# One list of token slots made apart from the others, maxima of k by pairwise operations, and a new hand order of a kernel's prologue

## The chip, the cores and the metric

The kernel runs on one core of a Trainium2 chip. A core has five engines, each with its own queue of instructions that it works off in order: TensorE (PE; matmuls and transpositions, with its weight loads shown as PEld), VectorE (DVE), ScalarE (ACT), GpSimd (POOL) and SyncE (SP, which here only issues DMAs). Engines wait for each other through semaphores. The metric is the device time of one execution in microseconds (us), and the number given for a kernel is a median over runs. The profile and the trace come from one profiled execution.

## The reference, cut to what matters

Three stages follow each other: a linear attention over 4 batches with 8 heads of 64 and 576 tokens, a mixture of 8 experts of which each of the 2304 tokens takes two, and a feed-forward stage with a rational function.

```python
q_s = softmax(q over head_dim)                     # q, k, v: (4, 8, 576, 64)
k_s = np.exp(k - np.max(k, axis=2, keepdims=True)) # the maximum over the 576 tokens
k_s = k_s / (k_s.sum(axis=2, keepdims=True) + 1e-9)
kv  = einsum('bhsd,bhse->bhde', k_s, v)
x   = einsum('bhsd,bhde->bhse', q_s, kv)           # -> (2304, 512)

noisy = x @ w_gate + log1p(exp(x @ w_noise)) * noise
top2  = the two largest of the 8 noisy logits of a token; weights: softmax over the two
for e in range(8): for k in range(2):
    mask = top2[:, k] == e
    out[mask] += weight[mask, k] * (relu(x[mask] @ w1[e]) @ w2[e])     # w1 512x1024, w2 1024x512

h = out @ w_in;  g = P(h) / (Q(|h|) + 1e-6);  return g @ w_out         # P cubic, Q quadratic
```

## The kernel before

**Stages.** The prologue (to about 127 us of the span) does the attention, the gate, the routing and expert 0's first 256 tokens. Then come expert 0's later tokens, experts 1 to 7 in blocks of up to 384 tokens, and the last stage. From the first block on, TensorE's queue is little else than matmuls, three for each product (lines 757 to 759: the operands are split into a high and a low part).

**The order.** In the prologue the order on every engine is written by hand: the string `ORDER` names steps (`name.index`), and each step appends its instructions to the queues of the engines that it uses. `LOADS` does the same for the first DMAs on SP's queue, and `REST` for what is left behind expert 0's `prep`. Behind the prologue a scheduler places instructions, and `issue_after` holds a group back behind a named mark.

**Steps of the attention.** Of a batch b, `km` holds 512 tokens of k as 128 partitions x (8 heads, 4 rows r, 64) and `kr` the 64 tokens left over. `krT`/`krm` find the leftover's maxima, `kmx` (L272) reduces the four rows r on VectorE, `kmT` transposes that on TensorE into a PSUM tile (`keyb`, which cycles through three), `kmm` reduces over partitions (L284, L285), `kmB` spreads the maxima into a PSUM tile `pm`, `ksb` subtracts them (`ek`, `kr`; L298, L301), `kex` takes exponentials on ScalarE (L305), `ksm` sums on POOL, `kv` multiplies with v (`pk`; weights are `vm` and `vr`), `kz`/`kvn` divide, `kvT`/`kvc`/`kg`/`kgc` make from it the matrix `kvx` that yields outputs and gate logits at once (`pg` is its gate part). For q, `qmx` (L369: `mx`), `qsb`, `qex`, `qsm` (`qs`), `qse`, `qrc` and `qnm` are the softmax. For each of 18 token tiles, `xT` transposes q (`qT`, two PSUM tiles), `xc` copies it on ScalarE (`qTs`), `xp` multiplies with `kvx` (`px`, one PSUM tile), `xo` copies the outputs on ScalarE, `xs` stores them to `Xrows` in DRAM and `xg` sums the gate logits `L` on VectorE (L458). `aw`, `sa` and `sv` load and split expert 0's weights (`w10h`, `w10l` and so on, in halves of 128x1024).

**Steps of the routing.** The tokens are taken in two halves, g = 0 and 1, of 9 tiles. `route` (`rt.g`) makes the noisy logits, the two largest, the counts (`rt`, L555, and the matmuls `base`), positions and then, in three groups of 3 tiles, one-hots on VectorE: `route<-route,itC` (L585) and `ocv` (L591) for the list's columns and `oh` (L594, 128x768) for its 128 rows. There are 48 columns: 6 for each of the 8 experts. `fill_list` (`rl.g`) multiplies them on TensorE into one `list` in PSUM (18 matmuls of 96 columns). From g = 0 come the indices `gidxA` of expert 0's first 256 tokens, from g = 1 the indices `gidxE` of its later 384 and, ordered by the experts' sizes (`ranks`), `gidx` for experts 1 to 7. `weights` (`rw.g`) makes the gate's weights.

**Expert 0.** `ag` gathers its first tokens (`xga`), `at`/`ac`/`al` transpose and split them (`xTa`, `xa`), `m1`/`mb` are the first product (`pha`), `mr`/`ml` its relu and split, `m2`/`mc` the second (`acca`). `eg` gathers the later ones (`xgb`), the first instruction of which on TensorE is `xT<-ident,xgb` (L803); VectorE splits these into `xl` (L806). Experts 1 to 7 gather by `gidx` (`xg<-Xrows,gidx`, L787), and their weights `raww` are loaded on SP and split by ScalarE (`w10h`, L678) and VectorE (`w10l`, L679).

Of the kernel before, what the change touches and what calls it, by code (L numbers as in the profile page):

```python
# [38 lines left out]
NCOL = E * CC  # L39
# [19 lines left out]
    kg.1 xc.5 xT.4 kgc.1 rsm.0 xp.7 xc.4 krm.1 qse.0 kv.0.3 qrc.0 xo.7 xg.7 qmx.2 xp.4 xo.4 qnm.0.0 kz.0 rmx.1
    xg.4 rnm.0 rex.1 kvn.0 xp.5 qsb.2 xg.5 kmT.3 kmT.2 qmx.3 kvT.0 rse.1 xT.0 xo.5 xT.8 kvc.0 xp.6 kmm.3 qsb.3  # L60
    xc.0 xg.6 aw.0.0 kmB.3 kmm.2 xo.6 kg.0 xc.8 rsm.1 ksb.3 kmB.2 kgc.0 qex.2 xp.0 qnm.0.3 xs.4 xo.0 xs.6 rnm.1
    xg.0 xT.3 kex.3 ksb.2 xp.8 xs.7 qnm.0.2 xs.0 qnm.0.1 xs.5 xT.2 qex.3 kv.3.0 aw.0.1 ksm.3 xg.8 qsm.2 kv.3.1
    xc.2 xo.8 qsm.3 qse.2 xp.2 xc.3 xs.8 kex.2 aw.1.0 xT.1 kv.3.2 qrc.2 xg.2 qnm.2.2 kz.3 qse.3 xo.2 qnm.2.3
# [1253 lines left out]
```

## Time and profile before

| | us |
|---|---|
| median of 3 runs | 975.9 (974.28 to 1564.1) |
| the profiled execution | 974.89 |
| its span, first to last instruction | 972.9 |
| TensorE busy in the span | 941.4 (97%) |
| VectorE busy | 757.7 (78%) |
| ScalarE busy | 591.0 (61%) |
| POOL busy | 281.7 (29%) |

A row of the timeline has the start, the duration, the engine, the line, the operation and out<-in; in brackets behind it stand the idle time of that engine just before and what ended it. `PEld` rows are TensorE's weight loads, `SPq` rows the issues of DMAs. Names are those of the program without the batch or tile number, so `px` is the projection of some tile.

### The profile page before, as it was taken

The page shows a single profiled execution, that of the slowest core. Times are in us where ns is not written, and L with a number is a line of the kernel's source. Part 1 is how long each engine was busy: PE and PEld are TensorE (multiplying, and loading weights), DVE is VectorE, ACT ScalarE, POOL GpSimd, SP SyncE. Part 2 cuts the span into 40 slices and gives each one's busy share as a digit, 9 for nine tenths or more (in the row PEclk, how much of TensorE's full clock was granted, in tenths as well). Part 3 has the DMA queues.
Part 4 walks back from the last instruction along what each step waited for, and adds up shares of the span by engine and source line. Part 5 has one row for each costly group of instructions (what it writes and reads, how often), then busy time and mean ns, then how long its engine had stood idle before and what let it go on. Part 6 is the DMA issues. An engine that isn't in the chain of part 4 may idle for free. (4 is left out here: it accounts for less than half of the span.)

```text
span 972.9 us, 15490 instructions
## 1 busy us (share of the span) xinstructions
PE 941.4 (97%) x5296; PEld 841.8 (87%) x5296; DVE 757.7 (78%) x1552; ACT 591.0 (61%) x1198; POOL 281.7 (29%) x276
## 2 busy tenths in 40 slices
PE   2999899999999999999999999999999999999998
PEld 1888788888988888888989999899899999998997
DVE  6876769676877878778831389989899898798795
ACT  2586245464645556455631387787787877787775
POOL 4888221221302121122121142222323232232221
PEclk9999999999999999999999999999999999999999
DMA  9982168675866758586676591230020000000001
GB/s 265 298 274 80 63 224 250 190 219 170 242 197 214 249 175 259 167 250 216 208 233 201 175 359 34 76 108 23 1 76 1 17 27 1 33 1 1 33 1 33
DMA packets 91147, 137.35 MB, mean 141 GB/s; under 512 B 15698, under 2 KB 44374, under 8 KB 91064
## 3 DMA queue, kind: packets, MB, share of 16 engines
q1 hardware_dynamic: 76536, 100.27, 33.5%
q0 software_dynamic: 14528, 36.05, 11.9%
q8 instruction: 42, 0.69, 0.3%
q14 instruction: 41, 0.34, 0.1%
HBM read 100.64 MB, written 36.05 MB: 141 GB/s over the span
## 5 line engine op out<-in xcount | busy, mean ns | idle before, releaser
L1172 POOL TENSOR_TENSOR hlr<-vr,hhr 128x384 fp32r<-128x384 f32 x95 | 105.1, 1110 | 287.6 <-ACT hhr L1171 212.1
L757 PE MATMUL phr<-xhr,wih 128*128 128x384 f32 x384 | 129.8, 338 | 0.0
L759 PE MATMUL phr<-xhr,wil 128*128 128x384 f32 x384 | 129.3, 337 | 0.0
L758 PE MATMUL phr<-xlr,wih 128*128 128x384 f32 x384 | 129.0, 336 | 0.0
L822 DVE SCALAR_TENSOR_TENSOR hl<-ph,hh 128x256 fp32r<-128x256 f32 (+4 forms) x120 | 56.4, 470 | 76.8 <-ACT hh L821 75.6
L821 ACT ACTIVATE hh<-ph 128x256 fp32r<-128x256 f32 (+4 forms) x120 | 50.4, 420 | 106.3 <-PE ph L759 106.2
L758 PE MATMUL accr<-wol,hhr 128*128 128x512 f32 x288 | 113.4, 394 | 0.0
L757 PE MATMUL accr<-woh,hhr 128*128 128x512 f32 x288 | 112.7, 391 | 0.0
L759 PE MATMUL accr<-woh,hlr 128*128 128x512 f32 x288 | 109.6, 395 | 0.0
L1160 DVE SCALAR_TENSOR_TENSOR sqr<-sqr,coef,abr 128x384 f32<-128x384 f32 x96 | 64.2, 668 | 35.3 <-ACT sqr L1159 35.3
L787 POOL DMA_INDIRECT xg<-Xrows,gidx x35 | 39.5, 1128 | 158.9 <-PE xT L803 156.5
L1155 ACT ACTIVATE vr<-phr,coef 128x384 f32<-128x384 f32 x96 | 64.1, 668 | 33.1 <-PE phr L759 25.1
L1167 DVE SCALAR_TENSOR_TENSOR sqr<-sqr,qone,abr 128x384 f32<-128x384 f32 x96 | 71.7, 747 | 9.4 <-ACT abr L1166 5.2
L749 POOL DMA_INDIRECT Yrows<-y,sidx x35 | 38.9, 1113 | 136.9 <-ACT y L842 128.6
L1165 ACT ACTIVATE abr<-sqr,qone 128x384 f32<-128x384 f32 x96 | 59.7, 623 | 26.4 <-DVE sqr L1160 26.2
L757 PE MATMUL ph<-xh,w11h 128*128 128x256 f32 (+4 forms) x240 | 75.3, 314 | 0.0
L757 PEld LDWEIGHTS phr<-xhr,wih 128*128 128x128 f32 x384 | 72.2, 188 | 3.3
L758 PEld LDWEIGHTS phr<-xlr,wih 128*128 128x128 f32 x384 | 72.1, 188 | 3.3
L757 PE MATMUL ph<-xh,w10h 128*128 128x256 f32 (+4 forms) x240 | 72.0, 303 | 1.0 <-ACTq L1087 1.0
L758 PE MATMUL ph<-xl,w10h 128*128 128x256 f32 (+4 forms) x240 | 72.6, 303 | 0.0
L759 PE MATMUL ph<-xh,w11l 128*128 128x256 f32 (+4 forms) x240 | 72.6, 302 | 0.0
L758 PE MATMUL ph<-xl,w11h 128*128 128x256 f32 (+4 forms) x240 | 72.4, 301 | 0.0
(293 smaller groups left out, 2621.1 us busy)
## 6 DMA issues: line engine op xcount, KB each, us to landing
raww<-in_moe_w_dram SPq DMA_DIRECT2D x56, 512.0 KB, 4.5
r64i<-in_moe_w_in_dram SPq DMA_DIRECT2D x32, 256.0 KB, 3.4
r64o<-in_moe_w_out_dram SPq DMA_DIRECT2D x32, 256.0 KB, 3.1
ylr<-Yrows SPq DMA_DIRECT2D x32, 256.0 KB, 3.1
qm<-in_q_dram SPq DMA_DIRECT2D x4, 1024.0 KB, 7.8
vm<-in_v_dram SPq DMA_DIRECT2D x4, 1024.0 KB, 8.1
raw<-in_moe_w_dram SPq DMA_DIRECT2D x4, 1024.0 KB, 7.9
Xrows<-xo SPq DMA_DIRECT2D x16, 256.0 KB, 2.3
```

The costliest lines, as they stand in the source:

```text
L749: st = G.indirect_dma_start(out=Y, out_offset=bass.IndirectOffsetOnAxis(ap=idx, axis=0), in_=yt, in_offset=None, bounds_check=2 * NTOK - 1 ...
L757: PE.matmul(o, ah, bh, start=first, stop=False)
L758: PE.matmul(o, ah, bl, start=False, stop=False)
L759: return PE.matmul(o, al, bh, start=False, stop=last).ins
L787: G.indirect_dma_start(out=g[0:self.rows(t)], out_offset=None, in_=X, in_offset=bass.IndirectOffsetOnAxis(ap=self.cols(gidxE, gidx, t), ax ...
L821: a_ = A.activation(hh, ph, AF.Relu)
L822: v_ = V.scalar_tensor_tensor(hl, ph, 0.0, hh.bitcast(F32), op0=ALU.max, op1=ALU.subtract)
L1155: A.activation(v, ph, AF.Identity, scale=coef[:, 3:4], bias=coef[:, 2:3])
L1160: V.scalar_tensor_tensor(sq, sq, coef[:, 5:6], ab, op0=ALU.mult, op1=ALU.add)
L1165: A.activation(r0, sq, AF.Ln, bias=qone)
L1167: V.scalar_tensor_tensor(sq, sq, qone, r0, op0=ALU.add, op1=ALU.mult)
L1172: (V if self.end and f == NF2 - 1 else G).tensor_tensor(gl, v, gh.bitcast(F32), op=ALU.subtract)
```

## The change

1. **Maxima of k.** `kmx` was one reduction over r. Now `kmp`, a copy on ScalarE, puts row 0 into a PSUM tile (`keyb`), and `kmx` takes three maxima on VectorE, two in place in PSUM and the last from PSUM to SBUF. The steps of batch 1 from `kmp` to `kex` are done in two halves of four heads, and the load of its v comes in two (`vm1a`, `vm1b`).
2. **Expert 0's list.** `route` now makes a position `sE` and a value `vE` of expert 0 alone (at most one of a token's two choices is expert 0, so one entry per token in place of two), one-hots `ohE` of 640 and 512 elements and `ocvE` with 6 columns. `fill_first` (`re.g`) is 9 matmuls of 12 columns into `listE`. `gidxA` and `gidxE` come from it.
3. **The other experts' list.** `general` (`rg.g`) makes the one-hots of the 42 columns left from the positions kept in `pos` and `idf`. `rl.g` multiplies as before (18 matmuls, 84 columns). `ranks` (`rk`) stays in the prologue. For g = 1 nearly all of `rg`, `rl` and the indices `gidx` (`by_rank`, `rf`) stand in `REST`, behind expert 0's `prep`. Tiles that now live longer come from a pool `late`.
4. **Order.** `ORDER` is another one throughout. `REST` is also held behind the marks V and A (VectorE's and ScalarE's last split of expert 0's later tokens).

The core of the diff:

```diff
-    kr0 km1a km1b qm1 km0 - qr0 - vm1 - vr0 - qm0 - vm0 - km2 - kr1 - km3 - qm2 - vm2 - vr1 qr1 qm3 vm3
+    kr0 km1a km1b qm1 km0 - qr0 - vm1a - vm1b - vr0 - qm0 - vm0 - km2 - kr1 - km3 - qm2 - vm2 vr1 qr1 qm3 vm3
...
 REST = """
-    ay.0 mc.6 mc.7 ay.1
+    ay.0 mc.6 mc.7 rg.1 ay.1 rl.1 rl.1 rg.1 rl.1 rg.1 rf
 """
...
+    def kmp(b, h=None):
+        hs = heads(h)[0]
+        t = once("kmp", b, h, lambda: keyb(f"kmp{b}").rearrange("p (h d) -> p h d", h=H))
+        A.activation(t[:, hs], km[b][:, hs, 0, :], AF.Copy)
...
-            V.tensor_reduce(t, km[b].rearrange("p h r d -> p h d r"), axis=AX.X, op=ALU.max)
...
+            for r in range(1, R):
+                V.tensor_tensor(x if r < R - 1 else t, x, src[r], op=ALU.max)
...
+        V.scalar_tensor_tensor(ti, sE, AWAY, pb[:, EA:EA + 1].to_broadcast([P, TP]), op0=ALU.add, op1=ALU.add)
...
+        V.tensor_tensor(ocE, over(tj, CC), itC[:, 0:CC].unsqueeze(1).to_broadcast([P, TP, CC]), op=ALU.is_equal)
...
+        for t0, t1 in ((0, TA), (TA, TP)):
+            V.tensor_tensor(oh[:, t0:t1], tr[:, t0:t1].unsqueeze(2).to_broadcast([P, t1 - t0, P]),
+                            itR.unsqueeze(1).to_broadcast([P, t1 - t0, P]), op=ALU.is_equal)
+            yield
...
+    def fill_first(g):
+
+        lists["E", g] = qTb(f"listE{g}")[:, 0:2 * CC]
+        oh, ocv = ehot[g]
+        for t0, t1 in ((0, TA), (TA, TP)):
+            for t in range(t0, t1):
+                PE.matmul(lists["E", g], oh[:, t, :], ocv[:, t].rearrange("p z c -> p (z c)"),
+                          start=(t == 0), stop=(t == TP - 1))
+            yield
+
+    def general(g):
...
+    def by_rank():
+
+        lr = late.tile([P, NR, CC, NR], F32, name="lr")
+        lw = late.tile([P, NR, CC], F32, name="lw")
...
+        slots(late, lw.rearrange("p r c -> p (r c)"), NR * CC, gidx, sidx, "m")
...
-    with tc.issue_after(marks["xT"]):
+    with tc.issue_after(marks["xT"]), tc.issue_after(marks["V"]), tc.issue_after(marks["A"]):
         rest(REST)
```

Lines behind the new functions have other numbers in the changed kernel (757 to 759 are 843 to 845 there, L458 is L490, L806 is L892).

**First place.** VectorE's queue in the middle of the attention, between the two reductions for batches 2 and 3 and the first `ek` behind them; a digit behind a name is the batch or, for `px`, the tile. Before:

```order
L272 TENSOR_REDUCE kmx2_347<-km2_168 128x512
L272 TENSOR_REDUCE kmx3_374<-km3_175 128x512
L385 TENSOR_REDUCE qs0_390<-eq0_325 128x32
...
L458 TENSOR_REDUCE L_110<-px7_418 128x16
L369 TENSOR_REDUCE mx2_437<-qm2_178 128x32
...
L458 TENSOR_REDUCE L_110<-px5_470 128x16
L369 TENSOR_REDUCE mx3_488<-qm3_190 128x32
L284 TENSOR_REDUCE mr1_425<-kmT3_478 128x4
L285 TENSOR_REDUCE m3_515<-mr1_425 128x4
...
L284 TENSOR_REDUCE mr1_425<-kmT2_483 128x4
L285 TENSOR_REDUCE m2_530<-mr1_425 128x4
...
L298 TENSOR_TENSOR ek3_543<-km3_175,pm3_525 128x8x4x64
```

In the changed kernel:

```order
L401 TENSOR_REDUCE mx0_373<-qm0_169 128x32
L295 TENSOR_TENSOR kmp2_387<-kmp2_387,km2_175 128x512 x2
L295 TENSOR_TENSOR kmx2_389<-kmp2_387,km2_175 128x512
...
L401 TENSOR_REDUCE mx2_429<-qm2_185 128x32
L295 TENSOR_TENSOR kmp3_422<-kmp3_422,km3_182 128x512 x2
L295 TENSOR_TENSOR kmx3_451<-kmp3_422,km3_182 128x512
L490 TENSOR_REDUCE L_113<-px7_459 128x16
...
L417 TENSOR_REDUCE qs0_483<-eq0_403 128x32
...
L313 TENSOR_REDUCE mr1_474<-kmT2_493 128x4
L314 TENSOR_REDUCE m2_510<-mr1_474 128x4
...
L401 TENSOR_REDUCE mx3_527<-qm3_196 128x32
L329 TENSOR_TENSOR ek2_550<-km2_175,pm2_522 128x8x4x64
```

The two reductions for batches 2 and 3 became two pairs of maxima, with `mx` of batches 0 and 2 ahead of them. Batch 3's `mx` stood ahead of both `kmm`, and its `ek` was the first; now batch 2 goes first, and batch 3's `mx` stands directly ahead of batch 2's `ek`.

**Second place.** VectorE's queue from the positions of the second half's tokens to the indices `gidxE` of expert 0's later tokens (`hla` is the split of expert 0's hidden values). Before:

```order
L585 TENSOR_TENSOR route_1054<-route_1054,itC 128x288
L591 TENSOR_TENSOR ocv_0_1201<-route_1054,vhl 128x6x48 x2
L594 TENSOR_TENSOR oh_0_1211<-route_1054,itR 128x768
L585 TENSOR_TENSOR route_1054<-route_1054,itC 128x288
L591 TENSOR_TENSOR ocv_6_1234<-route_1054,vhl 128x6x48 x2
L594 TENSOR_TENSOR oh_6_1244<-route_1054,itR 128x768
L585 TENSOR_TENSOR route_1054<-route_1054,itC 128x288
L591 TENSOR_TENSOR ocv_12_1254<-route_1054,vhl 128x6x48 x2
L594 TENSOR_TENSOR oh_12_1260<-route_1054,itR 128x768
...
L601 TENSOR_TENSOR lfg_1283<-list_1227,lvg_982 128x48
L604 SCALAR_TENSOR_TENSOR route_1054<-list_1227,lfg_1283 128x48
...
L148 SCALAR_TENSOR_TENSOR gidxE<-route_1054,lu_1061 128x6
```

In the changed kernel:

```order
L608 SCALAR_TENSOR_TENSOR route_1130<-sE_1140,base_1238 128x9
L610 TENSOR_SCALAR route_1130<-route_1130 128x9
L611 TENSOR_SCALAR route_1130<-route_1130 128x9
L612 COPY pbs_1268<-base_1238 128x16
L613 TENSOR_TENSOR route_1130<-route_1130,itC 128x54
L615 TENSOR_TENSOR ocvE_1273<-route_1130,vE_1141 128x9x6
L616 TENSOR_TENSOR ocvE_1273<-route_1130,vhl 128x9x6
L620 TENSOR_TENSOR ohE_1276<-route_1130,itR 128x640
...
L620 TENSOR_TENSOR ohE_1276<-route_1130,itR 128x512
...
L625 TENSOR_TENSOR lf_1137<-listE_1293,lvE 128x6
L628 SCALAR_TENSOR_TENSOR route_1130<-listE_1293,lf_1137 128x6
...
L150 SCALAR_TENSOR_TENSOR gidxE<-route_1130,lu_1136 128x6
```

Three groups of one-hots of 768 elements became one of small instructions and two one-hots `ohE` of 640 and 512.

**Third place.** VectorE's queue around the index `gidx` of experts 1 to 7. Before, in the prologue and ahead of expert 0's later tokens:

```order
L490 TENSOR_REDUCE cap_94<-rkt 128x7
L615 TENSOR_TENSOR lr<-lvg_1282,perm 128x294
L618 TENSOR_REDUCE lw<-lr 128x42
L147 TENSOR_SCALAR lum<-lw 128x42
L148 SCALAR_TENSOR_TENSOR gidx<-lw,lum 128x42
...
L993 SCALAR_TENSOR_TENSOR hla<-pha_1275,hha 128x256
L993 SCALAR_TENSOR_TENSOR hla<-pha_1308,hha 128x256
...
L1023 TENSOR_SCALAR coef<-coef 128x4
L806 TENSOR_TENSOR xl_2_1392<-xT_2_0_1393,xh_2_1391 128x4x128
```

In the changed kernel, inside expert 0's block of later tokens (`hl` is the split of its hidden values, `w10l` and `w11l` are splits of expert 1's weights):

```order
L892 TENSOR_TENSOR xl_2_1436<-xT_2_1_1444,xh_2_1435 128x4x128
...
L687 TENSOR_TENSOR oh_0_1413<-list_1394,itR 128x768
...
L687 TENSOR_TENSOR oh_6_1473<-list_1394,itR 128x768
...
L687 TENSOR_TENSOR oh_12_1497<-list_1394,itR 128x768
...
L908 SCALAR_TENSOR_TENSOR hl_2_0_1563<-ph_2_0_1549,hh_2_0_1562 128x384
...
L765 TENSOR_TENSOR w10l_1577<-raww_1_1578,w10h_1576 128x1024
...
L765 TENSOR_TENSOR w10l_1577<-raww_1_1618,w10h_1576 128x1024
L694 TENSOR_TENSOR lfg_1505<-list_1480,lv_135 128x42
...
L704 TENSOR_TENSOR lr<-lv_136,perm 128x294
L706 TENSOR_REDUCE lw<-lr 128x42
...
L765 TENSOR_TENSOR w11l_1679<-raww_1_1680,w11h_1678 128x1024
L150 SCALAR_TENSOR_TENSOR gidx<-lw,lum 128x42
```

The index moved from ahead of the first split `xl` to behind three one-hot groups, two splits of hidden values and three splits of weights.

## Rows read from the trace of the kernel before

**Rows 1.** Stretches: us, busy PE, PEld, DVE, ACT, POOL (count); clock, DMA share, GB/s

```profile
42.00:50.00 8.00, 6.15 (x28) 5.84 (x27) 6.65 (x12) 3.93 (x19) 5.29 (x3) 0.66 1.01 272
50.00:84.00 34.00, 32.87 (x247) 30.05 (x247) 26.56 (x82) 27.25 (x43) 30.62 (x23) 0.95 0.62 204
84.00:104.00 20.00, 16.14 (x126) 13.86 (x125) 10.88 (x36) 9.90 (x22) 15.15 (x10) 0.96 0.40 123
104.00:127.00 23.00, 21.67 (x154) 19.17 (x154) 21.33 (x98) 3.65 (x11) 3.79 (x5) 1.00 0.15 47
127.00:973.00 846.00, 840.84 (x4604) 752.62 (x4602) 659.76 (x1303) 529.89 (x1076) 200.19 (x186) 1.00 0.43 133
126.70:148.20 21.50, 21.25 (x113) 19.23 (x112) 14.40 (x36) 11.51 (x20) 4.46 (x5) 1.00 0.73 236
```

**Rows 2.** Timeline, the last projections before expert 0

```profile
97.18 0.48 PEld L431 LDWEIGHTS qT<-ident,eq 128*128 128x128 f32 x4
...
98.41 1.03 PEld L444 LDWEIGHTS px<-kvx,qTs 128*128 128x128 f32 x8 [0.75 <-DVE L L458]
...
99.75 0.60 ACT L363 ACTIVATE xo<-px 128x512 f32<-128x512 f32 x1 [1.08 <-issue]
...
100.65 1.25 PE L444 MATMUL px<-kvx,qTs 128*128 128x144 f32 x8 [0.99 <-DVE L L458]
...
103.72 0.39 PE L757 MATMUL pha<-xa,w10h 128*128 128x256 f32 x1 [0.95 <-ACT xa L968]
```

**Rows 3.** VectorE by line, 0 to 60 us: busy, mean ns | idle

```profile
L272 DVE TENSOR_REDUCE kmx<-km 128x512 f32<-128x2048 f32 x4 | 14.8, 3731 | 1.1 <-DMA km<-in_k_dram 1.1
L298 DVE TENSOR_TENSOR ek<-km,pm 128x2048 f32<-128x2048 f32 x4 | 9.1, 2270 | 0.0
L369 DVE TENSOR_REDUCE mx<-qm 128x32 f32<-128x2048 f32 x4 | 9.1, 2263 | 0.0
...
L301 DVE TENSOR_TENSOR kr<-kr,pm 64x512 f32<-64x512 f32 x3 | 2.1, 684 | 0.1
```

**Rows 4.** Timeline, the last q load and the products with v

```profile
40.83 2.18 SPq L195 DMA_DIRECT2D qm<-in_q_dram  x1
...
57.83 1.91 ACT L305 ACTIVATE ek<-ek 128x2048 f32<-128x2048 f32 x1
...
60.52 0.97 PEld L317 LDWEIGHTS pk<-vm,ek 128*128 128x128 f32 x8
...
62.02 0.97 PEld L317 LDWEIGHTS pk<-vm,ek 128*128 128x128 f32 x8
```

**Rows 5.** DMA issues of the page: count, KB each, us to landing

```profile
raww<-in_moe_w_dram SPq DMA_DIRECT2D x56, 512.0 KB, 4.5
...
qm<-in_q_dram SPq DMA_DIRECT2D x4, 1024.0 KB, 7.8
```

**Rows 6.** Timeline, the list of the second half and behind it

```profile
109.15 0.21 DVE L555 TENSOR_REDUCE rt<-route 128x8 bf16<-128x72 f32 x1
...
113.98 0.95 DVE L594 TENSOR_TENSOR oh<-route,itR 128x768 bf16<-128x768 int32 x1
...
115.46 0.43 PE L630 MATMUL list<-ocv,oh 128*128 128x96 bf16 x6
...
116.20 0.95 DVE L594 TENSOR_TENSOR oh<-route,itR 128x768 bf16<-128x768 int32 x1
...
120.65 0.17 DVE L148 SCALAR_TENSOR_TENSOR gidxE<-route,lu 128x6 int32<-128x6 f32 x1
...
125.33 0.20 DVE L148 SCALAR_TENSOR_TENSOR gidx<-lw,lum 128x42 int32<-128x42 f32 x1
...
126.70 1.04 PE L803 MATMUL xT<-ident,xgb 128*128 128x128 f32 x8
...
135.65 1.23 DVE L679 TENSOR_TENSOR w10l<-raww,w10h 128x1024 fp32r<-128x1024 f32 x1 [0.39 <-ACT w10h L678]
```

**Rows 7.** Gathers by gidx, 118 to 165 us

```profile
DMA to landing us min/median/max: 3.8/6.7/6.9
```

More of the change, by code (lines that the diff above doesn't have):

```diff
@@ L38 @@
 CC = 6
-NCOL = E * CC
+NCOL = (E - 1) * CC
+TA = 5
+AWAY = 8192.0
 G2E = 2 * E
@@ L59 @@
[L59 to L63, printed above, removed]
@@ L267, in over_r, with heads @@
             eng.tensor_tensor(t, t, src[r], op=op)
-    def kmx(b, eng=None):
-        t = st["kmx", b] = pw.tile([P, H, HD], F32, tag="kmx", name=f"kmx{b}", bufs=2)
-        if eng is None:
-            V.tensor_reduce(t, km[b].rearrange("p h r d -> p h d r"), axis=AX.X, op=ALU.max)
-        else:
-            over_r(eng, t, [km[b][:, :, r, :] for r in range(R)], ALU.max)
-    def kmT(b):
-        pt = st["kmT", b] = keyb(f"kmT{b}").rearrange("p (c t) -> p c t", c=NHP)
-        for c in range(NHP):
+    def heads(h):
+        return [slice(None)] * 3 if h is None else [slice(h * n, (h + 1) * n) for n in (H // 2, NHP // 2, 2 * P)]
@@ L279, in kmT, with pairs, kmm @@
+    def pairs(h):
+        return range(NHP)[heads(h)[1]]
+    def kmT(b, h=None):
+        pt = once("kmT", b, h, lambda: keyb(f"kmT{b}").rearrange("p (c t) -> p c t", c=NHP))
+        for c in pairs(h):
             PE.transpose(pt[:, c, :], half(st["kmx", b], c), ident)
-    def kmm(b):
-        m = st["m", b] = pw.tile([P, NHP], F32, tag="m", name=f"m{b}", bufs=2)
+    def kmm(b, h=None):
+        cs = heads(h)[1]
+        m = once("m", b, h, lambda: pw.tile([P, NHP], F32, tag="m", name=f"m{b}", bufs=2))
@@ new lines, in route @@
+        le = lists["E", g]
+        if g:
+            V.tensor_tensor(lf, le[:, CC:], lvE, op=ALU.add)
+        else:
+            V.tensor_copy(lf, le[:, CC:])
+        V.scalar_tensor_tensor(lvp, le[:, 0:CC], 64.0, lf, op0=ALU.mult, op1=ALU.add)
+        if g:
+            slots(None, lvp, CC, gidxE, sidxE, "e", (lt, lu))
+        else:
+            slots(None, lvp[:, 0:NA], NA, gidxA, sidxA, "a", (lt[:, 0:NA], lu[:, 0:NA]))
+            V.tensor_copy(lvE, lvp)
+        yield
+        V.tensor_copy(n1 if g else n0, pbs[:, E:])
@@ new lines, in general, with B_ @@
+    def general(g):
+        n = TP
+        ts_ = slice(g * TP, (g + 1) * TP)
+        bank = psR.tile([P, 512], F32, tag="r", name=f"list{g}")
+        at_ = [0]
+        def B_(*shape, dt=F32):
+            return part(bank, at_, shape, dt)
+        oc = B_(TH * 2, NCOL)
+        ov, cf = (B_(TP, 2) for _ in range(2))
+        ti, tr = (B_(TP, 2, dt=I32) for _ in range(2))
+        tj = late.tile([P, TP, 2], I32, tag="tj", name=f"tj{g}")
+        ov2 = late.tile([P, TP, 2], F32, tag="ov2", name=f"ov2{g}")
+        V.tensor_copy(ti, pos[:, ts_])
+        V.tensor_scalar(ov, pos[:, ts_], float(CC * P), 1000.0, op0=ALU.is_ge, op1=ALU.mult)
+        V.scalar_tensor_tensor(ov2, idf[:, ts_], float(CC), ov, op0=ALU.mult, op1=ALU.add)
```

233 lines of the change are left out of this document (129 added, 104 removed).

## The prediction

> **What bounds the kernel now.** I read the busy time of each engine by stretches first [rows 1]. From 127 us to the end TensorE works 840.8 of 846 us at full clock: this is a queue of matmuls with no gap to win, and the change doesn't touch it. What can move is when that queue starts. Before 127 us, TensorE is idle 1.85 us of the stretch 42 to 50 (its granted clock there is 0.66 in the mean, so part of it ran at the lower of its two levels, 1.2 GHz), 1.1 us of 50 to 84, 3.9 us of 84 to 104 and 1.3 us of 104 to 127: 8.2 us in all. So the prize is small beside 973 us, and a gain of over 2% (19.5 us, about what a measurement of this kernel can tell from no change) would need more than all these gaps and the time of the lower clock together.
>
> Then I read the timeline of the worst stretch, 96 to 104 us [rows 2]. One projection `px` follows the other every 2.24 us (98.41, 100.65), though its weight loads fill only 1.03 us: there is one PSUM tile for it, so each waits for ScalarE's copy `xo` and VectorE's sum `L` of the one before. A transposition `qT` (0.48 us) in between doesn't fill the wait of 0.99 us. The first matmul of expert 0 (`pha`) starts at 103.72, the first transposition of expert 0's later tokens (`xT<-xgb`) at 126.70 [rows 6]. Those two are the posts to compare.
>
> **The k maxima.** Each of the four reductions `kmx` takes 3.73 us on VectorE [rows 3]. They become one copy on ScalarE and three VectorE maxima of 128x512 with an operand in PSUM. The trace has no such maximum. The nearest rows are `kr<-kr,pm` (512 elements for 64 partitions, one operand in PSUM): 0.68 us, and from above `mx<-qm` at 2.26 us for 2,048 elements, 0.57 us per 512 with no start of its own. I take 0.68, three times 2.05 us, so 1.7 us less VectorE time per batch, bounds 1.4 to 2.0, and 0.6 us more of ScalarE (as one `xo`).
> The two reductions `kmx` and `mx` have the same 2,048 inputs per partition, in and out of order, and 3.73 against 2.26 us [rows 3]. The Trainium skill, VectorE: DVE Perf Modes (section: The perf-mode tier table (the rule you actually need)), has only the one-element-per-cycle mode for a reduction, whatever its layout. By that rule `kmx` would cost what `mx` costs and the change would save only 0.2 us per batch; the trace doesn't agree, and the sum goes by the rows.
>
> 6.8 us less of VectorE doesn't become 6.8 us of span, since the data are late. The last q arrives about 7.8 us after its issue at 40.83 [rows 4, 5], at 48.6; the halved v load puts one more issue ahead of it, so I take 49.2. Now I follow the new order: VectorE has `mx` of batch 3 in front of `ek` of batch 2 (first place shown). So 49.2 + 2.3 (`mx`) + 2.3 (`ek`) [rows 3] = 53.8, exponentials of 1.9 on ScalarE [rows 4] and, for the rest rows with a quarter of the elements, 0.6 (as one `xo`), and `pk` of batch 2 starts at 56.4. What is before that post (batch 1 by halves, `pk` of batch 1 some us earlier) gains nothing: those matmuls wait in line for `vr0`, and the order meets again at this load. Halving costs two more starts each of small instructions, at a time when TensorE has nothing else (its queue is empty until the loads come); without that cover it would be 1 us.
>
> **From there to expert 0.** Ledger of TensorE from 56.4: 8 `pk` at 1.50 (60.52 to 62.02) [rows 4] = 12.0; 14 `px` at 1.03, one of them (16 loads in place of 8) half as long again = 14.9; 9 `qT`, 2 `kvT`, `pm` and 2 `xTa` at 0.48 = 6.7; 2 `pz` and 2 `pg` at 0.97 (8 loads, as the first part of `pk`) = 3.9; 27 list matmuls at 0.07 (six in 0.43) [rows 6] and the counts 0.2 = 2.1. Sum 39.6, so 96.0 with no wait. Waits: between `px` the new order puts 1.5 us and more of `pk`, `pz`, `pg` in the first half, which covers the 1.2 us that a cycle leaves open; between the last six it has 0.9 to 1.0, so 5 times 0.3 = 1.4. `L` stands behind one-hots of up to 1 us in VectorE's queue three times: 1.4. ScalarE has halves of weights (twice an `xo`, so about 1.1 us each) ahead of `xo` and copies of `qT`: 1.5. Together 4.3: `pha` starts at 100.3 instead of 103.72, **-3.4 us**. Bounds: no waits at all, -7.7; the waits of the old order and a half-clock stretch as at 42 to 50 us, +1.
> POOL doesn't set this: weight halves (`w..l`) that stood ahead of its last `eq` now stand behind them, and its queue from 28 to 81 us is full but ahead of `px`. If it slipped by over 4 us, it would be late next.
>
> **Expert 0's own list.** The chain from the last `L` to the index `gidxE` now: counts ready at 109.36, three one-hot groups 2.2 us apart (113.98, 116.20), index at 120.82 [rows 6]. That is 11.5 us from counts to index. In the new order (second place) there are two one-hots of 0.8 and 0.65 us (640 and 512 elements, in ratio to 0.95 for 768) and some 16 small instructions of 0.2 us: about 6.3 us. But while this chain ran, TensorE had expert 0's first 256 tokens to do: in the stretch from 104 to 127 it is idle for 1.3 us in all [rows 1]. So 5 us off the chain are worth at most those 1.3 us. The chain now starts 3.3 us later against `pha`, as the last `px` is directly ahead of it, and the counts come at about 8 us behind `pha` where the queue asks at 7. I keep 0.3 us of waits: **-1.0 us**, bounds -1.3 and +1. The list matmuls are 27 per half instead of 18, 9 more at 0.07: **+0.6 us** (those of the first half stand in the ledger).
>
> **The others' list.** It goes behind expert 0's later tokens: VectorE makes three one-hot groups after the first splits there, and only then the ranks' index `gidx` (third place). Counted from the first `xT<-xgb`: two splits, group 1, third split, groups 2 and 3 = 11 us; then hidden halves and two weight splits of 1.23 us [rows 6], 15.3; list, product and sum 17.8. Ahead of `gidx` in the queue stands a third weight split, whose load can start only when the first split is through (13.2) and lands 4.5 us later [rows 5]; a copy on ScalarE (1.1) and VectorE's 1.23: 20.1, `gidx` at 20.4. The gather lands 3.8 to 6.9 us later, 6.7 in the middle [rows 7]: at 24.2 to 27.3. What TensorE has to do until it transposes these rows follows from the old stretch, first `xT<-xgb` to first `xT<-xg`, 126.70 to 148.20: 21.25 us busy [rows 1] for 45,056 columns (40 matmuls of 512, 60 of 384, 12 of 128), 0.47 ns each. The new order adds 5 of 512, 11 of 384 (3.2 us) and 18 list matmuls (1.3): 25.7. With the middle landing the wait is 1.4: **+1.4 us**, bounds 0 and, with a chain 1.5 us longer and the late landing, +3.1. Behind it wait all matmuls; before, this index was ready at 125.5 us [rows 6], 22 us ahead of its transpositions.
>
> **Sum** against the profiled execution, 974.9 us (span 972.9 and 2.0 around it; the median of the runs shown is 975.9, 0.1% above): 974.9 - 3.4 - 1.0 + 0.6 + 1.4 = **972.5 us**.
>
> **Rivals.**
> *The prologue closes up.* For it: the new order interleaves `pk` of batch 3 with `px`, and the largest gaps, those of 84 to 104 [rows 1], are from that cycle alone. Against: ScalarE and VectorE take turns in the same cycle. It gives 974.9 - 7.7 - 1.3 + 0.6 + 0.3 = 966.8, and up to 3 us less if batch 1's earlier start carries through the late loads.
> *Nothing moves.* The `px` cycle stays the pace, or TensorE's clock falls as it did at 42 to 50, where the row at 0.66 holds 1.85 us of idle time [rows 1]. The stretch cost 8 times 0.34 = 2.7 us of clock. Then `pha` starts at 103.7 as before: 974.9 - 1.0 + 0.6 + 1.4 = 975.9. The Trainium skill, TensorE: Matmul & The Clock Gate (section: Why this matters for your kernels), says that idle gaps between bursts of matmuls bring the half clock back. By that rule the new order, which waits for the last q in the same stretch, pays this 2.7 us again; the trace agrees for the old one.
> *Slower: the others' list is late.* Place: VectorE's queue in expert 0's second block. Each us that the gather lands behind those 25.7 us is one us of span, from 3.8 us on it eats the gain. For it: three loads and a split stand ahead of one small index, and a load of 1 MB took 7.8 us in the full stretch against 4.5 for half of it here [rows 5]. Against: the load of that stretch is light. If that load comes 4.5 us later, as one more load in line, 977.0; with a second such stall at the next expert, 980.
>
> **How the numbers follow.** Forecast 0.45 (its own range 968 to 975.5), closing up 0.22, nothing moves 0.20, late list 0.13. The range 963 to 979 leaves out a quarter of the second and a third of the last, about 0.1, and a little of a kind that I don't see. Of over 2% either way: a gain needs 19.5 us where gaps and clock hold some 13; a loss needs the late list to stall 23 us. So faster 0.02, same 0.95, slower 0.03.
>
> **What would show it.** `pk` of batch 2 at 56 us, `pha` at about 100, `xT<-xgb` 21 to 22 us behind it; in 84 to `pha` idle time of TensorE under 3 us; the gather of expert 1's rows as the releaser of a wait of 1 to 3 us. The k copies and maxima at 0.6 and 0.68 us. I'm wrong if `pha` starts before 97 or after 104, or if TensorE waits over 4 us behind 127 us.

## The result: 967.2 us, and where TensorE gained it

The changed kernel takes 967.24 us (median, 966.12 to 968.49) against 976.09 before: a ratio of 0.9907, 95% interval 0.9883 to 0.9931. A second set of runs gave 967.49 us and a ratio of 0.9931 (0.9917 to 0.9945). So it is faster by 0.7 to 0.9%, 7 to 9 us: clear of no change, though less than the 2% that the prediction set as the size of a change. One of the four executions before took 1564.1 us and doesn't enter the ratio. The profiled execution took 968.49 us with a span of 966.6 (before 974.89 and 972.9).

The stretches of the changed kernel (columns as in [rows 1]: length, busy TensorE, weight loads, VectorE, ScalarE, POOL with counts; granted clock; DMA share; GB/s):

```profile
24.00:42.00 18.00, 17.96 (x118) 15.81 (x117) 14.21 (x18) 8.13 (x11) 14.96 (x11) 0.95 1.14 314
42.00:50.00 8.00, 7.31 (x46) 6.90 (x45) 5.99 (x9) 5.53 (x10) 5.62 (x3) 0.69 0.99 299
50.00:84.00 34.00, 32.33 (x252) 28.61 (x251) 27.66 (x85) 29.45 (x58) 32.18 (x25) 1.00 0.60 205
84.00:104.00 20.00, 18.74 (x161) 17.14 (x160) 16.50 (x80) 9.89 (x21) 14.29 (x9) 1.00 0.37 120
104.00:127.00 23.00, 22.17 (x145) 19.19 (x144) 19.98 (x78) 5.36 (x13) 4.90 (x5) 1.00 0.29 92
127.00:966.60 839.60, 834.28 (x4578) 746.94 (x4576) 659.14 (x1301) 527.96 (x1071) 199.03 (x184) 1.00 0.43 133
...
56.86:98.04 41.18, 38.93 (x317) 35.18 (x317) 32.87 (x120) 32.42 (x66) 39.39 (x28) 1.00 0.54 181
98.04:117.60 19.56, 19.42 (x141) 17.54 (x140) 15.47 (x89) 4.32 (x14) 3.69 (x5) 1.00 0.18 54
117.60:143.65 26.05, 25.36 (x148) 22.57 (x146) 21.61 (x54) 11.63 (x19) 5.22 (x5) 1.00 0.57 197
```

From 127 us to the end TensorE is idle for 5.3 us, as before (5.2). All that changed lies ahead. In 84 to 104 it is idle for 1.3 us in place of 3.9 [rows 1]; 50 to 104 runs at full clock, where before it was 0.95 and 0.96; but 24 to 50 has the lower clock again (0.95 and 0.69, so part of it ran at the lower of the two levels, 1.2 GHz). The posts in the timeline (start, duration, engine, line, operation, out<-in, count, idle time before and what ended it):

```profile
21.66 1.91 PE L349 MATMUL pk<-vm,ek 128*128 128x128 f32 x8
...
50.45 2.23 DVE L401 TENSOR_REDUCE mx<-qm 128x32 f32<-128x2048 f32 x1
...
56.86 1.16 PE L349 MATMUL pk<-vm,ek 128*128 128x128 f32 x8
...
98.07 0.37 PE L843 MATMUL pha<-xa,w10h 128*128 128x256 f32 x1
...
105.17 0.23 DVE L592 TENSOR_REDUCE rt<-route 128x8 bf16<-128x72 f32 x1
...
111.95 0.17 DVE L150 SCALAR_TENSOR_TENSOR gidxE<-route,lu 128x6 int32<-128x6 f32 x1
...
117.60 0.60 PE L889 MATMUL xT<-ident,xgb 128*128 128x128 f32 x4
...
122.54 0.79 PE L843 MATMUL ph<-xh,w10h 128*128 128x384 f32 x3 [0.69 <-ACT xh L891]
...
135.72 0.20 DVE L150 SCALAR_TENSOR_TENSOR gidx<-lw,lum 128x42 int32<-128x42 f32 x1
...
143.65 0.60 PE L889 MATMUL xT<-ident,xg 128*128 128x128 f32 x4
```

The first product with v (`pk`) starts at 21.66 us, 1.8 us earlier than before:

```profile
23.49 1.92 PE L317 MATMUL pk<-vm,ek 128*128 128x128 f32 x8
```

`pk` of batch 2 starts at 56.86, expert 0's first matmul (`pha`) at 98.07 in place of 103.72 [rows 2], its later tokens (`xT<-xgb`) at 117.60 in place of 126.70 [rows 6], and the first rows of expert 1 are transposed at 143.65, with no wait in front.

To compare kernels by these posts, I split the time from the first `pk` to the first `pha` into TensorE's idle time, the time that the lower clock took (one less the granted clock, summed over stretches from 24 us on) and the rest, which is work at full clock. All in us, each from one profiled execution:

| kernel | first `pk` | first `pha` | idle | clock | rest | span |
|---|---|---|---|---|---|---|
| before | 23.5 | 103.7 | 6.9 | 5.1 | 68.2 | 972.9 |
| changed | 21.7 | 98.1 | 3.7 | 3.4 | 69.3 | 966.6 |
| changed, second profile | 22.4 | 97.0 | 4.2 | 1.7 | 68.7 | 965.5 |
| changed, maxima by reductions | 24.3 | 100.4 | 4.8 | 1.7 | 69.6 | 968.8 |
| the same, second profile | 23.3 | 99.3 | 5.8 | 1.7 | 68.5 | 967.7 |
| changed, batch 1 whole | 23.4 | 97.0 | 4.7 | 0.0 | 68.9 | 965.9 |
| changed, logits from the copy | 21.9 | 97.2 | 5.2 | 1.7 | 68.4 | 965.6 |
| changed, product first | 18.5 | 100.8 | 8.4 | 1.7 | 72.2 | 969.3 |
| changed, q's maximum behind | 19.5 | 102.9 | 5.9 | 10.2 | 67.3 | 971.6 |
| before, pairwise maxima | 22.5 | 102.2 | 9.9 | 3.4 | 66.4 | 972.0 |
| before, logits from the copy | 23.4 | 105.6 | 12.3 | 1.7 | 68.2 | 975.8 |

From before to changed, `pha` comes 5.6 us earlier: 1.8 from the start, 3.2 from idle time, 1.7 from the clock, and 1.1 lost to more work in the stretch. From `pha` to the end the program is 0.65 us shorter (869.18 and 868.53 us), of which 0.24 us is idle time. The second profile splits its 6.7 us into 1.1, 2.7, 3.4 and 0.5 lost: the clock's share differs from one execution to the next, that of the idle time hardly does.

What the clock took can also be estimated for every execution, as the span times one less its mean granted clock (means over a kernel's executions; the clocks are recorded to 0.001, about 1 us). For the kernel before that is 3.6 to 4.0 us in four sets of runs, for the changed kernel 1.9 and 2.3 us in its two. So of the 7 to 9 us some 1.5 to 2 are the clock, and most of the rest is start and idle time.

### The profile page after: what moved, and what is told of

Read it like the earlier page. It is cut to its first block, busy times and chain, and to the rows that moved or that the text cites. A ratio compares the mean times of both kernels' runs of the same rounds, so it can differ in the third digit from the quotient of the medians.

```text
span 966.6 us, 15583 instructions
## 1 busy us (share of the span) xinstructions
PE 939.6 (97%) x5314; PEld 839.6 (87%) x5314; DVE 757.2 (78%) x1591; ACT 594.7 (62%) x1205; POOL 281.6 (29%) x276
## 5 line engine op out<-in xcount | busy, mean ns | idle before, releaser
L1259 POOL TENSOR_TENSOR hlr<-vr,hhr 128x384 fp32r<-128x384 f32 x95 | 105.6, 1115 | 286.9 <-ACT hhr L1258 221.4
L1252 ACT ACTIVATE abr<-sqr,qone 128x384 f32<-128x384 f32 x96 | 59.7, 623 | 25.7 <-DVE sqr L1247 25.5
L843 PEld LDWEIGHTS phr<-xhr,wih 128*128 128x128 f32 x384 | 72.2, 188 | 3.3
L843 PE MATMUL ph<-xh,w10h 128*128 128x256 f32 (+4 forms) x240 | 72.2, 303 | 1.8 <-ACTq L1174 1.1
```

What stands on the lines that cost most here:

```text
L843: PE.matmul(o, ah, bh, start=first, stop=False)
L1252: A.activation(r0, sq, AF.Ln, bias=qone)
L1259: (V if self.end and f == NF2 - 1 else G).tensor_tensor(gl, v, gh.bitcast(F32), op=ALU.subtract)
```

## The experiments

Two theories stood at the start. One is the prediction's: the order of the projections pays, and VectorE's time for the maxima is lost in later waits. The rival: VectorE's time pays. A third question is what the place of the others' list is worth.

**Pairwise maxima alone, in the kernel before.**

```diff
+    def kmp(b):
+        t = st["kmp", b] = psR.tile([P, 512], F32, tag="r", name=f"kmp{b}").rearrange("p (h d) -> p h d", h=H)
+        A.activation(t, km[b][:, :, 0, :], AF.Copy)
...
+            for r in range(1, R):
+                V.tensor_tensor(x if r < R - 1 else t, x, km[b][:, :, r, :], op=ALU.max)
...
 ORDER:  kmx.b  ->  kmp.b kmx.b
```

> The kernel before, with only the maxima of k changed: a copy on ScalarE into PSUM (the routing's bank, which is free until the routing) and three maxima on VectorE, batch 1 whole, old order. VectorE has 6.6 us less to do before 43 us (four times 3.73 against 2.07). If the order of the projections is what paid (my theory), nothing behind 56 us moves by more than 1 us: the products with v of batch 3 still start at 60 us, expert 0 at 103, and the time is 974 to 976. If VectorE's time is what paid (rival), the first of them start 1.7 us or more earlier and the time falls to 970 or lower.

975.67 us, ratio 0.9996 (0.9981 to 1.0012): no difference. The first `pk` came 1.0 us earlier, and a wait behind it grew. Before, and in this run:

```profile
44.55 2.29 PE L444 MATMUL px<-kvx,qTs 128*128 128x144 f32 x8 [1.85 <-DVE L L458]
```

```profile
47.06 0.69 DVE L427 TENSOR_REDUCE mxr<-qr 128x8 f32<-128x512 f32 x1 [2.58 <-DMA qr<-in_q_dram]
...
47.93 2.29 PE L452 MATMUL px<-kvx,qTs 128*128 128x144 f32 x8 [3.56 <-DVE L L466]
```

Before, this wait of a projection for VectorE's sum `L` was 1.85 us; here it is 3.56. VectorE isn't busy there: ahead of `L` in its queue stands the maximum of q's leftover rows, and it waits 2.58 us for their load. In the old order what the maxima save is given back at this place. That is what the prediction said of them (the data are late), for the order that they were not made for. `pha` does come 1.5 us earlier in this profile, but the table has 1.7 us less of the lower clock there.

**The new parts in the old order.** The changed kernel, with the old `ORDER` and `LOADS`, batch 1 whole, and the new list steps where the old ones stood.

```diff
 ORDER (changed kernel's steps in the old order; k copies in the routing's bank; routing steps only):
-    rt.0 rl.0 rt.0 rt.0 rl.0 ...
+    rt.0 re.0 re.0 rt.0 rt.0 rw.0 ... rg.0 rg.0 rl.0 rg.0 rl.0 rg.0 rl.0 rg.0
```

> The changed kernel's parts (pairwise maxima, expert 0's own list, the others' list behind expert 0's later tokens) under the old prologue order and the old order of loads, with batch 1 whole. The new list steps stand where the old ones stood. Theory: the parts give only the 1.2 us of waits that TensorE has between expert 0's first matmul and its later tokens, less 0.6 us for nine more list matmuls: 974 to 975.5, with the first matmul of expert 0 at 103 to 104 us. Rival (the parts carry the gain, the order only fits them): 967 to 970. In between would split the gain.

989.72 us, ratio 1.0134 (1.0112 to 1.0155). Neither theory had that. Ahead of expert 0, TensorE stands in front of the others' one-hots:

```profile
96.16 0.60 PE L699 MATMUL list<-ocv,oh 128*128 128x84 bf16 x6 [6.00 <-DVE oh L668]
98.27 0.60 PE L699 MATMUL list<-ocv,oh 128*128 128x84 bf16 x6 [1.51 <-DVE oh L668]
...
112.43 0.38 PE L824 MATMUL pha<-xa,w10h 128*128 128x256 f32 x1 [0.95 <-ACT xa L1035]
```

VectorE now makes expert 0's list first, and the others' comes that much later, while its matmuls stand in TensorE's queue where the old list stood. So I placed the others' list of the first half by hand between and behind the last projections:

```diff
 ORDER:
-    ... rg.0 rg.0 rl.0 rg.0 rl.0 rg.0 rl.0 rg.0 ... ag.0 ... xg.16 ... xg.9 xs.9 ... xg.10 at.1 rt.1 at.0 ...
+    ... ag.0 rg.0 ... xg.16 rg.0 ... xg.9 rg.0 xs.9 rl.0 ... xg.10 rg.0 at.1 rl.0 at.0 ac.1 ac.0 al.1 al.0 rl.0 rg.0 rt.1 ...
```

> The changed kernel's parts under the old prologue order, as in the run that took 989.7, but with the others' list of the first half later, so that TensorE doesn't stand in front of its one-hots (it waited 6.0 and 1.5 us there): the one-hots lie between the last projections on VectorE, the list's matmuls behind them on TensorE. Theory (parts without the new order are worth only what they save of waits behind expert 0's start, 1.2 us): 974 to 976. Rival (they carry most of the gain when placed well): 970 or less.

985.96 us, 1.0120 (1.0102 to 1.0137), which neither theory had either. `pha` is back at 106.1, 2.4 us later than before, since the one-hots now delay `L`, and the projections with it:

```profile
91.76 1.25 PE L457 MATMUL px<-kvx,qTs 128*128 128x144 f32 x8 [2.16 <-DVE L L471]
...
105.88 0.41 PE L699 MATMUL list<-ocv,oh 128*128 128x84 bf16 x6 [1.24 <-DVE oh L668]
...
129.38 0.60 PE L699 MATMUL list<-ocv,oh 128*128 128x84 bf16 x6 [3.47 <-DVE oh L668]
```

But that is the small part. The span of this profile is 12.0 us longer than before (984.9), and 9.6 us of it lie behind `pha`. There TensorE waits 1.6 us for the gathered later tokens, then the row at 129.38 for the second half's one-hots, with matmuls of expert 0 behind it in the queue, and from 127 to 150 its granted clock is 0.85. The first placement has the same wait of 3.47 us and the same 0.85 there: of its 16.0 us, 7.3 lie behind `pha`. In both, the matmuls of the second half's list stand in `REST` as in the changed kernel.

So these two placements, both by hand, cost more than they save, in both halves: the list apart is more work for VectorE where TensorE waits for VectorE. That it can pay only with the new order is not shown by them, as a better place in the old order was not looked for.

**Maxima by reductions again, in the changed kernel** (run twice).

```diff
     def kmp(b, h=None):
+        return
```

> The changed kernel with the maxima of k done by reductions again (no copy on ScalarE; batch 1 still by halves), everything else and the order as in the changed kernel. VectorE gets 1.6 us more per batch. In the changed kernel VectorE waits 1.3 us behind the maxima of batch 2 and 1.9 us behind those of batch 3, so I expect the two late ones to vanish in these waits, and the early ones to be covered by the late loads: 967 to 968.5, expert 0's first matmul at 98 to 99 us. Rival (VectorE's time is the gain): 971 to 974, first matmul at 102 or later.

970.53 us, 0.9937 (0.9915 to 0.9959).

> The changed kernel with the maxima of k by reductions, once more, since its first ratio (0.9937, interval 0.9915 to 0.9959) does not part it from the changed kernel (0.9907 and 0.9931 in two sets of runs), while its trace has expert 0's first matmul at 100.4 us in place of 98.1 and 97.0. Theory (TensorE works without a gap from its first product with v on, so the reduction of batch 0 ahead of it, 1.6 us longer, and the two of batch 1 ahead of that show in full): first product at 24 to 25 us, expert 0 at 99.5 to 101, ratio 0.995 to 0.997. Rival (the offset is lost in waits, and the first trace was a chance of the clock): expert 0 at 97 to 98.5, ratio 0.992 to 0.9935.

969.60 us, 0.9945 (0.9928 to 0.9961). The intervals of the ratios overlap those of the changed kernel, but the times don't: its ten lie between 966.1 and 968.5 us, these twelve between 969.3 and 971.9. They were taken on several chips, on which the kernel before differs by up to 2 us, and by the ratios the difference is 0.6 to 3.7 us. Less the estimate of the clock the means are 967.2 us in both sets, against 965.3 in both sets of the changed kernel. So the maxima are worth about 2 us in the new order, and nothing that the runs can show in the old one (0.4 us, interval from 1.9 gained to 1.2 lost). The trace says why. In the changed kernel, and in the second of these runs:

```profile
20.78 1.09 PE L307 MATMUL kmT<-ident,kmx 128*128 128x128 f32 x4 [6.37 <-DVE kmx L295]
```

```profile
22.39 1.09 PE L308 MATMUL kmT<-ident,kmx 128*128 128x128 f32 x4 [7.77 <-DVE kmx L298]
...
46.76 1.22 PE L477 MATMUL px<-kvx,qTs 128*128 128x144 f32 x8 [1.58 <-DVE L L491]
```

Batch 0's transposition `kmT` waits for VectorE 7.77 us (6.37 in the changed kernel), and all products with v stand behind it on TensorE. Mean `pha` of the two is at 99.9, of the changed kernel's two profiles at 97.5. Of these 2.3 us, 1.75 are the later start and 1.4 more idle time, less 0.85 of clock (table). The wait at 46.76 for `L`, behind the longer reduction of batch 3, is one that I had expected to be none.

**Batch 1 in one piece.**

```diff
 ORDER:  kmp.1.0 ... kmp.1.1 ... kex.1.1  ->  kmp.1 ... kex.1, each at the place of its second half
```

> The changed kernel with the steps of batch 1 from the copy to the exponentials done in one piece, at the place of their second half (its v still loaded in halves). The products with v of batch 1 start about 2 us later. Theory: all of it is lost again in front of the products of batch 2, which wait for the last q (56.9 us in the changed kernel): 967 to 968. Rival (the early start carries through): 969 to 971.

968.63 us, 0.9922 (0.9900 to 0.9944): not to be told from the changed kernel. The first `pk` is at 23.4, `pha` at 97.0, but this execution had no stretch at the lower clock, so its profile can't decide whether the halves' 1.0 to 1.7 us arrive at the end. Less the estimate of the clock its six runs are at 966.7 us in the mean, 1.4 above the changed kernel, which speaks for it; from one set of runs that stays open.

**The others' list early.** In the changed kernel, the second half's general list moved from `REST` into the prologue.

```diff
 ORDER:
-    ... mb.6 rk m2.5 ... rg.1 mc.4 m2.7 rg.1 mc.5
+    ... mb.6 rk rg.1 rg.1 rg.1 rl.1 rg.1 rl.1 m2.5 ... mc.4 m2.7 mc.5 rl.1 rg.1 rf
 REST:
-    ay.0 mc.6 mc.7 rg.1 ay.1 rl.1 rl.1 rg.1 rl.1 rg.1 rf
+    ay.0 mc.6 mc.7 ay.1
```

> The changed kernel with the other experts' list of the second half back in the prologue: its one-hots and matmuls directly behind the ranks, ahead of expert 0's later tokens, the index at the prologue's end. VectorE gets 6.6 us of one-hots between the splits of expert 0's hidden values. The prediction had a wait of 1.4 us for the late list; the trace of the changed kernel has at most 0.5 us of idle time in that stretch. Theory: the place of the list is worth nothing by itself where it is now, and in the prologue it delays the splits, on which TensorE waits: +1 to +4 us, 968 to 971. Rival (late list costs its 1.4 us, VectorE has room in the prologue): 966.

978.69 us, 1.0027 (1.0016 to 1.0038): 11 us slower than the changed kernel, more than either theory had. `pha` is at 98.7 as there; then

```profile
119.36 0.91 PE L870 MATMUL xT<-ident,xgb 128*128 128x128 f32 x4 [2.31 <-DVE ov L651]
123.74 0.60 PE L699 MATMUL list<-ocv,oh 128*128 128x84 bf16 x6 [3.47 <-DVE oh L668]
125.85 0.60 PE L699 MATMUL list<-ocv,oh 128*128 128x84 bf16 x6 [1.51 <-DVE oh L668]
...
122.74 0.95 DVE L668 TENSOR_TENSOR oh<-list,itR 128x768 bf16<-128x768 int32 x1
```

TensorE waits 2.3, 3.5 and 1.5 us for the list's arithmetic and one-hots, and its clock falls (0.80 in 108 to 127). The wait is larger than I had expected because I had counted VectorE's time only, and not that the list's matmuls stand in TensorE's queue between expert 0's.

**Logits summed from ScalarE's copy**, so that a projection's PSUM tile has one reader in place of two. In both kernels `xo` had to be moved ahead of `xg` for some tiles (six in the changed one, seven in the one before).

```diff
-        t = pw.tile([P, 2, 2, 2 * HD], F32, tag="xo", name=f"xo{T}", bufs=5)
-        copy(eng, t, px[:, :, :, 0:2 * HD])
+        t = pw.tile([P, 2, 2, NV], F32, tag="xo", name=f"xo{T}", bufs=5)
+        copy(eng, t, px)
...
-        V.tensor_reduce(L[:, T, :], st["px", T][:, :, :, 2 * HD:]...
+        V.tensor_reduce(L[:, T, :], st["xo", T][:, :, :, 2 * HD:]...
```

> The changed kernel, but ScalarE's copy of a projection takes the gate logits along (576 columns in place of 512, about 0.66 us), and VectorE sums them from that copy in SBUF. So the one PSUM tile of the projections comes free after one reader in place of two that follow each other (0.60 and then 0.22 us). Theory (this chain sets the distance of two projections where little else lies between them): in the changed kernel TensorE waits 2.2 us between 56.9 and 98 us, about half of it behind such a sum; 1 us less, 966 to 966.8. Rival (the waits are for other things by now): no change, 967.2 or, with stores from a copy that isn't contiguous any more, slower.

967.78 us, 0.9919 (0.9901 to 0.9937): no change.

> The same edit in the kernel before, under its own order. There four waits of TensorE behind such a sum, between 93 and 101 us, add up to 2.3 us, in cycles of 2.24 us. Theory: the cycle falls to about 2.0 us, expert 0's first matmul comes 1.5 to 2.5 us earlier, and the time is 973.5 to 974.5. Rival (the cycle is set by ScalarE, which also copies the transposed q): no change, 976.

978.51 us, 1.0034 (1.0018 to 1.0049): 3 us slower. The cycle of projections did fall, from 2.24 to 1.99 us (97.70 to 99.69), but other waits took its place:

```profile
43.60 1.25 PE L426 MATMUL px<-kvx,qTs 128*128 128x144 f32 x8 [1.58 <-ACT xo L345]
...
53.77 0.62 PE L272 MATMUL pm<-ident,m 128*128 128x128 f32 x4 [2.10 <-DVE m L267]
...
66.18 0.63 PE L413 MATMUL qT<-ident,eq 128*128 128x128 f32 x4 [1.68 <-ACT qTs L417]
...
97.70 1.25 PE L426 MATMUL px<-kvx,qTs 128*128 128x144 f32 x8 [0.30 <-ACT xo L345]
...
99.69 1.25 PE L426 MATMUL px<-kvx,qTs 128*128 128x144 f32 x8 [0.30 <-ACT xo L345]
```

`pha` is at 105.6, 1.8 us later than before. So the cycle that I read as the limit of 84 to 104 is one of several: shortened by itself, and with seven copies placed ahead of other work on ScalarE, it brings nothing.

**Two attempts at the start.** After the run with reductions I thought that the start of TensorE's queue sets its end, and tried to bring it forward; the changed kernel was run beside them.

> The changed kernel itself, unchanged, on the same chip as the next three, so that they can be compared with it. Both theories: 0.990 to 0.991 of the kernel before.

967.49 us, 0.9931 (0.9917 to 0.9945).

```diff
 ORDER (product first):        kmT.0 kv.1.0  ->  kv.1.0 kmT.0
 ORDER (q's maximum behind):   qmx.1 kmp.0 kex.1.1 kmx.0  ->  kmp.0 kex.1.1 kmx.0 qmx.1
```

> The changed kernel with one step of its order moved: the first product of batch 1 (eight weight loads of v's first half and two of the rest) stands ahead of the transposition of batch 0's maxima on TensorE, which waits there 6.4 us for VectorE (to 20.8 us). New theory (behind its first product TensorE has a queue without gaps to the end of the prologue, so the start of that product sets everything): the product starts when its v has landed, some time between 19 and 21 us in place of 21.7, and what follows comes earlier by as much as it overlaps that wait, 0 to 1.5 us: 966 to 967.2. Rival (the last q's load or POOL set the later part): no change or, as the transposition is delayed by the product, up to 1 us slower.

971.19 us, 0.9971 (0.9956 to 0.9985).

> The changed kernel with batch 1's maximum of q (2.29 us) moved behind batch 0's maxima of k on VectorE, and so out of the way of the transposition with which TensorE's unbroken work begins at 20.8 us. New theory: that transposition starts 2.3 us earlier, at 18.5, the first product with it if its v has landed (19 to 21 us), and the end comes 1 to 2 us earlier: 965 to 966.5. Rival (POOL, busy 39.4 of the 41.2 us from 56.9 to 98, is the next limit, and the exponentials of q that it starts come 2.3 us later): no change or slower by up to 2 us.

970.97 us, 0.9965 (0.9951 to 0.9979). Both did bring the first product forward, to 18.5 and 19.5 us, and both are slower than the changed kernel beside them, by 3.7 and 3.5 us. With the product first:

```profile
18.55 2.04 PE L330 MATMUL pk<-vm,ek 128*128 128x128 f32 x8 [3.36 <-DMA vm<-in_v_dram]
21.81 0.77 PE L330 MATMUL pk<-vr,kr 64*128 64x128 f32 x2 [1.22 <-DMA vr<-in_v_dram]
...
33.85 1.13 PE L330 MATMUL pk<-vm,ek 128*128 128x128 f32 x8 [1.56 <-DVE kvx L353]
```

The data are not there yet (3.36 and 1.22 us of waits for v), batch 0's transposition comes 1.0 us later (22.51 against 21.50), and 1.56 us go at 33.85, where a product waits for `kvx`. With q's maximum behind:

```profile
18.58 1.09 PE L288 MATMUL kmT<-ident,kmx 128*128 128x128 f32 x4 [4.05 <-DVE kmx L276]
...
29.67 1.87 PE L342 MATMUL pz<-ones,ks 128*128 128x1 f32 x8 [2.59 <-POOL ks L324]
...
30.00:38.00 8.00, 8.00 (x41) 7.19 (x40) 5.01 (x8) 1.09 (x2) 7.76 (x6) 0.63 1.13 324
...
38.00:42.00 4.00, 4.00 (x32) 3.64 (x32) 1.81 (x6) 0.18 (x1) 3.56 (x3) 1.00 1.16 265
...
42.00:50.00 8.00, 7.31 (x36) 6.70 (x34) 6.23 (x8) 5.25 (x8) 5.42 (x3) 0.54 0.94 284
50.00:57.00 7.00, 7.00 (x51) 6.62 (x51) 5.50 (x7) 4.44 (x7) 2.94 (x4) 0.79 0.40 146
```

TensorE starts 2.9 us earlier than in the run beside it and then waits 2.59 us at `pz` for POOL's sums `ks`, since POOL's subtraction for q, ahead of these sums, came later (20.72 against 19.26). Behind this wait the granted clock is 0.63; from 38 to 42 it is 1.00, and then it falls a second time, to 0.54 and 0.79, without a wait in front. This profile is of the slowest of the six executions (973.48 us), but the lower clock is in all of them: 0.989 to 0.996, against 0.997 and 0.998 in the changed kernel beside it. Estimated as above it took 7.3 us in the mean, against 2.3. That is more than the 3.5 us by which this kernel is slower: without the clock it would be about 1 us ahead. With the product first the clock isn't the reason (3.3 us); there the waits are.

So the start counts only as far as POOL keeps up (in the second profile of the changed kernel the sums are ready at 28.2 us and asked for at 29.9) and as far as the clock holds. My theory of the start alone falls. The pairwise maxima help by bringing batch 0's `kmx` forward for TensorE: with reductions `kmT` starts at 22.39 and 23.37 us, against 20.78 and 21.50. POOL's subtraction for q, behind batch 1's maxima, moves little (18.74 and 19.73 us with reductions, 18.53 and 19.26 without).

None of these kernels beats the changed one. Two were not made: the new order with one list for all experts, and the lists apart at a place found for the old order. So the maxima's part of the gain is measured, and how the rest divides between the order and expert 0's own list stays open.

## Why the prediction held, and where its steps failed

The range (963 to 979) holds the time and the direction is right, but 972.5 is 5.3 us above the median, and 4.0 above the profiled execution (968.5), for which it was reckoned. The median is just below the forecast's own range (968 to 975.5), and at the rival in which the prologue closes up (966.8): the range held because it took this rival in. Step by step:

*Prices of the maxima: right.* VectorE by line in the changed kernel, to 60 us (mean ns behind the busy time):

```profile
L295 DVE TENSOR_TENSOR kmp<-kmp,km 128x512 f32<-128x512 f32 x6 | 4.2, 700 | 0.2
...
L295 DVE TENSOR_TENSOR kmx<-kmp,km 128x512 f32<-128x512 f32 x3 | 2.1, 692 | 0.1
```

0.70 and 0.69 us, forecast 0.68. And the reduction in the run with reductions again took 3.7 us, as in [rows 3]. Why it takes more than `mx` for the same 2,048 inputs is not shown: the order of the inputs differs, but so does the number of results (512 against 32).

*"What is before that post gains nothing": wrong.* This is the step that failed in its reasoning. `pk` of batch 2 did start at 56.86 (forecast 56.4), but not because the last q landed late: its maximum `mx` started at 50.45 right behind other work in VectorE's queue, and in the second profile, 0.7 us later in the beginning, at 49.37, when the load, issued at 41.41, had landed 6.7 us later, at 48.1. That the post came out where it was forecast is luck. TensorE's queue of the new order runs from its first product on with waits of 0.7 us at most until 67, and none of them is for `vr0`, at which the prediction had the order meet again. So what the maxima save ahead of it arrives at the end: about 2 us by the runs with reductions.

*Waits from there to expert 0: too large.* The sum had 39.6 us of work and 4.3 of waits from this post to `pha`. The stretch 56.86 to 98.04 has 38.9 busy and 2.25 idle. The 2 us are the largest single error of the sum, with the 0.7 of work. (Its 5 times 0.3 is 1.5, not 1.4.)

*The clock: taken at full speed, without saying so.* The work from 56.4 on was priced at full clock, and so it ran (1.00 from 50 to 104). The old order had lost 2.5 us from 50 on (0.95 and 0.96 in [rows 1]), 1.9 of it behind 56.4. That this would be won is not in the sum; only the last paragraph on the chances counts the clock. The rival in which nothing moves reckoned that the lower clock would take its 2.7 us ahead of 50 again, and there it took 3.4 and 1.7 in the two profiles: right, but no reason for `pha` to stay where it was. The Trainium skill, TensorE: Matmul & The Clock Gate (section: Why this matters for your kernels), names idle gaps as what brings the half clock back. For the first fall in the run with q's maximum behind that agrees (a wait of 2.59 us, then 0.63). For the second fall there and for the changed kernel it does not, below.

*Expert 0's own list: right.* Counts at 105.40, index at 112.12: 6.7 us (forecast 6.3; the terms that it names make 4.7, and four splits `hla` of 0.41 us stand in the queue between them). Idle time from `pha` to the later tokens fell from 1.3 to 0.1 us (forecast: 1.0 gained).

*The others' list: no wait.* The index was ready 18.3 us behind `xT<-xgb` (forecast 20.4), and TensorE had 25.4 us of work (25.7) in the 26.05 until it transposed the gathered rows, without a wait for them. So the gather was covered, and the 1.4 us fell away. In the one other place that was tried, the run with the list early, it cost 11 us.

So 972.5 less 2.0 and 0.7 (waits and work of the stretch), less 1.4 (the list), and 0.2 more of the first list, plus 0.5 of a later post, is 968.7; the profiled execution took 968.5.

*The signs.* `pk` of batch 2, the idle time from 84 us to `pha` and the prices came out as said. Three did not: `pha` is at 98.1 and 97.0 (about 100; the second is at the bound of 97 that the prediction had set itself), no gather of expert 1's rows holds TensorE up, and `xT<-xgb` comes 19.5 us behind `pha` where 21 to 22 were named. The last had left out work that the prediction itself puts behind that post: the 18 list matmuls (1.3 us) and, as an estimate from its 0.47 ns per column, 1.2 us for five matmuls of 512.

## What to carry to other kernels

An instruction's time is worth what stands behind it in the queues: the same edit to the maxima gave nothing that the runs could show in one order, where VectorE then waited for a load, and about 2 us in the other, so cost an edit together with the order that comes with it. When a post comes out where it was forecast, still ask what held it; a wait in a queue and a late load look the same until the row ahead on that engine is read. And when the first matmul of a dense queue is moved forward, look for the second engine that feeds it (here POOL): past its pace the gain turns into a gap. Compare the granted clock of all runs as well: here it took 5 us more where the start had won 2.9, and only part of that stood behind the gap.
